# One SBUF arena, one PSUM pool and interleaved hand-overs between the four stages of a pre-LN recurrent-memory transformer block with its gradients

## The chip, the cores and the metric

The kernel runs on one core of a Trainium2 chip. The metric is the device time of one execution in microseconds (us), as the median of several executions; lower is better. A core has TensorE (PE; its weight loads are listed apart as PEld), VectorE (DVE), ScalarE (ACT), GpSimd (POOL) and SyncE (SP). They run their own instruction streams in order and meet at semaphores. SP and POOL also issue transfers (DMAs), which 16 DMA engines carry out.

## The reference

x is 2048 x 448, in bf16. A pre-normalised attention with a recurrent memory is followed by a gated feed-forward network (FFN), and the outputs are the result and the gradients for x, the first memory and seven weights:

```python
for s in range(n_seg):                       # 64 segments of 32 tokens, memory of 8 rows
    h = jnp.concatenate([mem, xs], axis=1)   # 40 rows
    q, k, v = h @ Wq, h @ Wk, h @ Wv         # 16 heads of 256
    p = softmax(mask(q k^T * scale))
    o = (p v) @ Wo
    mem = o[:, :M, :]                        # next segment needs this one
h = x + A(layernorm(x))
h2 = h + (silu(n @ w_gate) * (n @ w_up)) @ w_down      # n = layernorm(h)
# out: h2, and the vjp of all of it for grad_out
```

The memory makes the attention a chain over 64 segments forward and 64 segments backward.

## The kernel before

One scheduler mode is used throughout: the program's text is the order of each engine's instructions. The work has four stages, one after the other.

- **Forward** (`forward_chain`): 64 segments s, grouped by four into 16 token tiles t of 128 rows. Each segment projects K, Q and V (L471, L479), shifts V into the layout of the attention (V_sb, through POOL copies at L437 and SP transfers from Vev at L667), and multiplies by Wo (L600). A tile's output steps (o_units: u1, e1, u2, u3, e3, ut, et) are spread over the following segments; `out_ev` stores a tile of h (Hh, L653).
- **FFN**, forward and backward of it together (`ffn_phase`): 16 tiles t. Per tile: load h and grad_out, `norm`, `hn_turn` (L978), `gate`, `up`, `slope`, turn z (L1036), `dz` (dout times w_down transposed, L996 with its 64-row rest L999), `down_mm` (L1050), `grads`, `dh_turn` (L1036), `dh_mm` (L1079, both halves of the gradient of the normalised input), `dh_ln` and `dh_out` (L1096). `mm_d` works in pairs of 448-column banks: three chunks of 128 rows, then the last 64 rows from two halves of the partitions.
- **Backward** (`backward_chain`): segments 63 down to 0, with do_units (L1191) per tile and projections by the transposed weights WvT, WkT, WqT (L1218). WoT and WvT are loaded during the FFN, WkT and WqT (`load_back`, L926) after segment 63's own loads.
- **Tail** (`tail_phase`): 22 phases of weight gradients (L1674, L1689), six for the FFN and 16 for attention, with memory turns (`mem_turn`: load memld, transpose at L1663, store) inside the first two phases.

Big weights live in `wall`, four regions W[0] to W[3] that the stages reuse. Every stage opens its own SBUF pools and its own PSUM pool (6 banks + 2 fixed in forward and backward, 8 banks in FFN and tail), and is written out wholly before the next one begins.

The FFN's weights for its backward half come by `load_rest`, called at the head of `ffn_phase`. It is all on SP's queue, in this order: w_down (Wd, L905), three transposes of 128 columns of w_down (L907), a transpose of the last 128 columns (L908), a copy that puts the last 64 of them at partitions 0 to 63 of the fourth chunk (L909), then the transposes of w_gate (L910) and w_up (L911).

Of the kernel before, what the change touches and what calls it, by code (L numbers as in the profile page):

```python
# [18 lines left out]
class _Prio:  # L19
# [5 lines left out]
    def crit(self):  # L25
        from contextlib import contextmanager

        @contextmanager
        def _cm():
            off = self.tc.cur_priority - self.next  # L30
            with self.tc.high_priority(offset=off):
                yield
                self.next = self.tc.cur_priority
        return _cm()

# [147 lines left out]
def run_all(k: _K):  # L183
# [89 lines left out]
    with tc.tile_pool(name="wfwd", bufs=1) as wf, \  # L273
            tc.tile_pool(name="psA", bufs=6, space=bass.MemoryType.PSUM) as psa, \
            tc.tile_pool(name="psS", bufs=1, space=bass.MemoryType.PSUM) as pss:
        k.pspool = psa
        k.s_ps = [pss.tile([P, 512], FP32, name=f"s_ps{i}") for i in range(2)]
        for i in range(2):
            nc.vector.memset(k.s_ps[i][:], 0.0)
        Wk_sb, Wq_sb, Wv_sb = [W[i].rearrange("p (c n) -> p c n", c=KC) for i in range(3)]  # L280
        Wo_sb = W[3][:, 0:MC * D].rearrange("p (c d) -> p c d", c=MC)
        NWIN = 8
        hA = wf.tile([P, KC, NWIN, SEG], BF16)
        memT_all = W[3][:, MC * D:KC * HD].rearrange("p (c s m) -> p c s m", c=KC, s=NSEG)
        k.memT_all = memT_all
        maskf = wf.tile([L, L], FP32)
        nc.gpsimd.memset(maskf[:], 0.0)
        nc.gpsimd.affine_select(out=maskf[:], in_=maskf[:], compare_op=ALU.is_ge, fill=-1e9 / k.scale,
                                base=0, pattern=[[-1, L]], channel_multiplier=1)
        nc.gpsimd.memset(maskf[0:M, :], 0.0)  # L290
        maskr = wf.tile([L, H // 2 * L], BF16)
        for hh in range(H // 2):
            nc.vector.tensor_copy(out=maskr[:, hh * L:(hh + 1) * L], in_=maskf[:])
        k.part = wf.tile([P, DP], FP32, name="part")
        k.partB = wf.tile([P, DP], FP32, name="partB")
        nc.vector.memset(k.part[:], 0.0)
        nc.vector.memset(k.partB[:], 0.0)

        with tc.tile_pool(name="workA", bufs=2) as work, tc.tile_pool(name="stageA", bufs=1) as stage:
            order = ExitStack()  # L300
            order.enter_context(tc.manual_schedule())
            DB = D // 4
            m0f = work.tile([P, DP], BF16, name="m0", tag="xtmp", bufs=2)
            m0 = m0f[0:M, :]
            nc.sync.dma_start(out=m0[:, 0:D], in_=MEM0)
            Xs = W[3][:, 0:NT * D].rearrange("p (t d) -> p t d", t=NT)
            XNs = W[3][:, NT * D:2 * NT * D].rearrange("p (t d) -> p t d", t=NT)
            xv = X2.rearrange("(t p) d -> p t d", p=P)
            xnv = XN.rearrange("(t p) d -> p t d", p=P)
            for q in range(4):  # L310
                nc.sync.dma_start(out=Xs[:, 4 * q:4 * q + 4, :], in_=xv[:, 4 * q:4 * q + 4, :])
            for Wt, Wsrc in ((Wk_sb, Wk2), (Wq_sb, Wq2), (Wv_sb, Wv2)):
                wv = Wsrc.rearrange("(a j p) n -> a p j n", a=2, j=2)
                for a in range(2):
                    nc.sync.dma_start(out=Wt[0:DB].rearrange("p (j a) n -> p j a n", a=2)[:, :, a, :], in_=wv[a])
            pm = ps1(BF16)
            for kc in range(KC):
                w0 = (kc % 2) * 2 * DB + (kc // 2) * DB
                nc.tensor.transpose(pm[0:DB, kc * M:(kc + 1) * M], m0[:, w0:w0 + DB], ident[0:M, 0:M])
            k.evac(hA[0:DB, :, 0, 0:M], pm[0:DB, 0:KC * M].rearrange("p (c m) -> p c m", m=M), "v")  # L320
            nc.scalar.copy(out=memT_all[0:DB, :, 0, :], in_=hA[0:DB, :, 0, 0:M])
            mv1 = small.tile([P, NT, 2], FP32, name="mv1", bufs=1)
            sd1 = small.tile([P, NT], FP32, name="sd1", bufs=1)

            def norm_rows(out, t):
                nc.vector.tensor_scalar(out=out, in0=Xs[:, t, :], scalar1=mv1[:, t, 0:1], scalar2=rstd1[:, t:t + 1],
                                        op0=ALU.subtract, op1=ALU.mult)

            def first_rows(t):
                xl = work.tile([P, DP], BF16, name="xload", tag="xload", bufs=1)  # L330
                norm_rows(xl[:, 0:D], t)
                return xl

            def norm_group(q):
                ts = range(4 * q, 4 * q + 4)
                for t in ts:
# [7 lines left out]
            def store_group(q):  # L344
                for t in range(4 * q, 4 * q + 4):
                    norm_rows(XNs[:, t, :], t)
# [60 lines left out]
def forward_chain(k: _K, hA, NWIN, Wq_sb, Wk_sb, Wv_sb, Wo_sb, maskr, work, stage, ff):  # L407
# [289 lines left out]
    for s in range(NSEG):  # L697
# [44 lines left out]
        if s == NSEG - 1:  # L742
            ff.load_first()
# [186 lines left out]
def ffn_phase(k: _K, W, ff, work, mv2, rstd2, srcs):  # L930
# [194 lines left out]
    for t in range(NT):  # L1125
        if t + 2 < NT:
            load(t + 2)
# [715 lines left out]
```

## Time and profile before

| | us |
|---|---|
| median of 3 executions | 3030.61 (3029.78 to 3058.03) |
| the profiled execution's own time | 3044.81 |
| its span in the profile | 3043.0 |
| TensorE busy in that span | 2775.7 (91%) |
| VectorE, ScalarE, GpSimd busy | 1501.9, 1164.3, 737.2 |

The profiled execution was 14.2 us longer than the median; 1.8 us of it lie outside the span. Its mean granted TensorE clock was 0.971 of full speed.

The windows view, cut at the stages and at the seams between them (window, length, busy time and instruction count of each engine, granted TensorE clock, busy share of the DMA engines, GB/s):

```profile
65.00:980.00 915.00, 864.63 (x17644) 500.54 (x17640) 536.28 (x1683) 424.81 (x1130) 216.42 (x463) 0.99 0.40 125
980.00:1045.00 65.00, 39.63 (x384) 19.67 (x373) 25.78 (x58) 24.54 (x48) 8.14 (x15) 0.79 0.93 247
1045.00:1110.00 65.00, 62.71 (x436) 32.54 (x435) 47.38 (x80) 35.64 (x61) 16.27 (x25) 0.97 0.79 177
1110.00:1290.00 180.00, 180.00 (x1289) 95.76 (x1288) 138.12 (x234) 109.47 (x188) 38.11 (x72) 1.00 0.32 116
1345.00:1410.00 65.00, 31.75 (x474) 16.16 (x471) 17.99 (x44) 13.73 (x38) 7.98 (x18) 0.66 0.92 200
1410.00:2310.00 900.00, 846.88 (x19553) 485.11 (x19549) 533.66 (x1425) 430.53 (x1414) 228.11 (x466) 0.99 0.58 159
2310.00:2395.00 85.00, 67.40 (x684) 34.86 (x685) 16.73 (x44) 13.41 (x35) 24.62 (x43) 0.96 0.88 310
2395.00:3043.00 648.00, 615.31 (x3614) 310.85 (x3648) 123.01 (x233) 71.00 (x104) 175.33 (x241) 0.98 1.04 194
```

The first number after the length is TensorE (PE), then PEld, DVE, ACT, POOL. The stages proper are lines 1, 4, 6 and 8; lines 2, 5 and 7 are the seams forward to FFN, FFN to backward and backward to tail, and line 3 is the FFN's first tiles. In a timeline line the columns are start, length, engine, source line, operation, output and inputs, count, and in brackets the idle time before it with what ended it. The page's list of queues gives the queue of SP's transfers as a whole:

```profile
q1 hardware_dynamic: 577920, 297.58, 44.3%
```

That is packets, MB, and the time the packets took as a share of 16 engines' span.

### The profile page before, as it was taken

Reading aid. Unit: us, or ns where it says so; the run is one execution under the profiler, and the core shown is the slowest. Engines: PE = TensorE matmul, PEld = TensorE weight load, DVE = VectorE, ACT = ScalarE, POOL = GpSimd, SP = SyncE. Lnnn points to the kernel's source line nnn. Section 1 sums busy time; section 2 is a strip of 40 time slices with the busy share of each in tenths; the row PEclk is TensorE's granted clock in tenths of the full one; section 3 lists DMA queues with packets and bytes.
Section 4 is the critical chain, followed back from the end, with each engine's and each line's share of the span. In section 5 each row is a group of like instructions: output and inputs, shape, how many; then the busy total and the mean of one; then the engine's idle time right before and its main releaser. Section 6 shows DMA issues by size and latency. Waiting matters only on the chain.

```text
span 3043.0 us, 105017 instructions
## 1 busy us (share of the span) xinstructions
PE 2775.7 (91%) x44548; PEld 1530.2 (50%) x44584; DVE 1501.9 (49%) x3931; ACT 1164.3 (38%) x3087; POOL 737.2 (24%) x1388
## 2 busy tenths in 40 slices
PE   3999999999998799986999999999997999998989
PEld 1555555555554355543555555555554454444544
DVE  3555655565555577763556655656553112111211
ACT  1444444444443456652444544544442011110100
POOL 1222222222222122221222222222222223322232
PEclk7999999999999899997999999999999999999999
DMA  9343444434444763358655665665576999999995
GB/s 252 113 129 122 129 125 126 128 123 129 129 125 141 205 157 119 123 151 178 176 144 146 183 158 150 181 160 142 149 194 227 287 211 213 194 207 188 188 199 119
DMA packets 626771, 496.14 MB, mean 163 GB/s; under 512 B 487168, under 2 KB 538960, under 8 KB 616768
## 3 DMA queue, kind: packets, MB, share of 16 engines
q1 hardware_dynamic: 577920, 297.58, 44.3%
q0 software_dynamic: 48384, 191.85, 19.5%
q8 instruction: 352, 5.77, 0.8%
q14 instruction: 115, 0.94, 0.1%
HBM read 137.63 MB, written 222.08 MB: 118 GB/s over the span
## 4 chain that ended last, share of the span: by engine, by line
PE 71%; DMA 8%; DVE 7%; issue 6%; SPq 3%; ACT 3%; POOL 1%; another core or an unknown queue 0%; POOLq 0%; ACTq 0%; DVEq 0%
PE psf L1689 12%; PE psf L1218 9%; PE psf L471 9%; PE psf L1191 4%; PE psf L600 4%; DMA V_sb<-Vev 3%; PE psf L479 3%; PE psf L1494 3%; PE psf L1674 3%; PE psf L996 3%; PE psh L485 2%; PE psf L1702 2%; PE psf L1079 2%; DMA wall<-in_A_Wv_dram 2%; PE pob L1218 2%
## 5 line engine op out<-in xcount | busy, mean ns | idle before, releaser
L1689 PE MATMUL psf<-wall,H_all 128*128 128x512 bf16 x1404 | 322.1, 382 | 17.2 <-DMA wall<-dQA 11.7
L471 PE MATMUL psf<-wall,hA 112*32 112x512 bf16 x4096 | 233.4, 380 | 17.0 <-DVE hA L529 15.2
L1689 PEld LDWEIGHTS <-H_all 128*128 128x128 bf16 x1440 | 139.8, 98 | 183.2 <-issue 27.3
L1601 DVE CAST resc<-psf 128x512 bf16<-128x512 f32 (+1 forms) x58 | 39.0, 673 | 322.9 <-PE psf L1689 288.8
L471 PEld LDWEIGHTS <-hA 112*32 112x32 bf16 x4096 | 103.5, 97 | 129.8 <-DVE hA L529 31.3
L1599 ACT CAST resc<-psf 128x512 bf16<-128x512 f32 (+1 forms) x54 | 31.0, 573 | 334.4 <-PE psf L1689 297.0
L1545 POOL COPY dmem<-dA 128x32 bf16<-128x32 bf16 x63 | 13.2, 210 | 558.6 <-DVE dA L1230 558.6
L437 POOL COPY V_sb<-Vev 32x512 bf16<-32x512 bf16 x128 | 77.2, 603 | 275.1 <-ACT Vev L434 271.3
L1182 DVE COPY partC<-psf 128x224 f32<-128x224 f32 x64 | 25.0, 391 | 230.6 <-ACT partC L1185 230.6
L1191 PE MATMUL psf<-wall,dA 128*32 128x512 bf16 x2048 | 122.4, 381 | 13.0 <-DVE dA L1230 13.0
L1674 PE MATMUL psf<-dOut_all,wall 128*128 128x448 bf16 x640 | 127.1, 358 | 7.6 <-DMA wall<-OTA 7.6
L479 PE MATMUL psf<-wall,hA 112*32 112x512 bf16 x2048 | 134.0, 382 | 0.0
L1674 PEld LDWEIGHTS <-wall 128*128 128x128 bf16 x864 | 84.5, 99 | 95.9 <-issue 14.3
L1218 PE MATMUL psf<-wall,dkA 128*32 128x448 bf16 x2048 | 113.8, 364 | 18.6 <-DMA wall<-in_A_Wk_dram 13.1
L1218 PE MATMUL psf<-wall,dqA 128*32 128x448 bf16 x2048 | 113.2, 362 | 14.9 <-DMA wall<-in_A_Wq_dram 10.6
L1182 DVE COPY dO_sb<-dOev 32x512 bf16<-32x512 bf16 x256 | 121.2, 474 | 7.0
L1218 PE MATMUL psf<-wall,dvA 128*32 128x448 bf16 x2048 | 122.2, 358 | 0.4
L600 PE MATMUL psf<-wall,oA 128*32 128x224 bf16 x4096 | 116.7, 269 | 0.0
L1218 PE MATMUL pob<-wall 128*32 128x448 bf16 x1536 | 108.1, 358 | 1.7 <-issue 1.7
L1185 ACT CAST dOev<-psf 128x512 bf16<-128x512 f32 x64 | 37.5, 585 | 183.2 <-PE psf L1191 182.0
L1185 ACT CAST wall<-psf 128x64 bf16<-128x64 f32 x512 | 106.7, 247 | 0.0
L471 PE MATMUL psf<-wall,hB 112*32 112x512 bf16 x1024 | 75.6, 397 | 30.1 <-DMA wall<-in_A_Wk_dram 18.6
(284 smaller groups left out, 5792.5 us busy)
## 6 DMA issues: line engine op xcount, KB each, us to landing
Vtok<-V_sb SPq DMA_DIRECT2D x128, 192.0 KB
KtokA<-Kev SPq DMA_DIRECT2D x64, 256.0 KB
QtokA<-Qev SPq DMA_DIRECT2D x64, 256.0 KB
OTA<-oA POOLq DMA_DIRECT2D x16, 1024.0 KB, 6.0
Q_sb<-QtokA SPq DMA_DIRECT2D x128, 128.0 KB
K_sb<-KtokA SPq DMA_DIRECT2D x128, 128.0 KB
dVA<-dvA POOLq DMA_DIRECT2D x16, 1024.0 KB, 5.1
dKA<-dkA POOLq DMA_DIRECT2D x16, 1024.0 KB, 7.3
```

The source lines that it names most:

```text
L437: nc.gpsimd.tensor_copy(out=out, in_=in_)
L471: nc.tensor.matmul(ps[32 * g:32 * g + 32, :], lhsT=stat(kc), rhs=W_sb[0:DB, kc, c0:c0 + HB], start=(kc == 0), stop=(kc == KC - 1))
L479: nc.tensor.matmul(ps[32 * g:32 * g + 32, :].rearrange("t (y d) -> t y d", y=2), lhsT=stat(kc), rhs=wv[:, x, :, half, e, :], start=(kc == ...
L600: nc.tensor.matmul(ps[32 * g:32 * g + 32, 0:2 * DB], lhsT=x, rhs=Wo_sb[:, c, a * 2 * DB:(a + 1) * 2 * DB], start=first, stop=last)
L996: nc.tensor.matmul(out[b][:, 0:BW], lhsT=xT[:, kc, :], rhs=Wx[:, kc, f0:f0 + BW], start=(kc == 0), stop=False)
L1182: nc.vector.tensor_copy(out=out, in_=in_)
L1185: nc.scalar.copy(out=out, in_=in_)
L1191: nc.tensor.matmul(ps[32 * g:32 * g + 32, :], lhsT=stat(kc), rhs=WoT_sb[:, kc, c0:c0 + HB], start=(kc == 0), stop=(kc == KC - 1))
L1218: nc.tensor.matmul(pO[32 * g:32 * g + 32, 0:D], lhsT=ch(c), rhs=WT[:, c, :], start=(first and i < 4), stop=(last and i >= MC - 4), skip_gr ...
L1494: nc.tensor.matmul(po[:, n * L:(n + 1) * L], lhsT=lhs[b:b + L, lc:lc + P], rhs=rhs[b:b + L, hh, 0:L], start=True, stop=True)
L1674: nc.tensor.matmul(ps[:, 0:D], lhsT=stat[:, i, c * P:(c + 1) * P], rhs=Y[:, i, 0:D], start=(i == 0), stop=(i == kts - 1))
L1689: nc.tensor.matmul(ps[:, 0:N], lhsT=Hx[:, i, dc * P:(dc + 1) * P], rhs=X[:, i, b * N:(b + 1) * N], start=(i == 0), stop=(i == kts - 1))
```

## The change

**One arena.** All stages' buffers are views of one SBUF tile of 77,824 bytes per partition, at offsets written out as text per stage; a buffer waits only for those it overlaps. There is one PSUM pool of six rotating banks and two fixed ones (forward's scores; the FFN's pf and pdh; backward's scores and pob). FFN and tail so have 6 rotating banks instead of 8. The FFN's sg, u and z get two buffers, and slope works in place.

**Stages as generators.** `ffn_phase` is stepped from inside forward's last segment (`next(feed)`), backward from the FFN's last tiles (`next(back)`), and the tail from backward's last segment (`next(tails)`).

```diff
+        final = s == NSEG - 1
+        if final:
+            next(feed)                       # load(0), load(1)
...
-        v_shift(V_sb, Vev, 0, (2, 3), D_)
+        v_shift(V_sb, Vev, 0, (2, 3), A if final else D_)
...
-        v_shift(V_sb, Vev, 1, (0, 1), D_)
+        v_shift(V_sb, Vev, 1, (0, 1), G_ if final else D_)
...
         p_ev(1, 1, V)
+        if final:
+            next(feed)                       # rstd(0, NT - 1), norm(0)
...
             nc.sync.dma_start(out=dr["Vtok"][s, gg], in_=V_sb[QB * gg:QB * gg + 48, :])
+        if final:
+            next(feed)                       # load_rest
...
             if half == 1:
                 cur["u3"]()
+                if final:
+                    next(feed)               # hn_turn(0)
...
-    late2["et"]()
-    late["ut"]()
-    late["et"]()
-    u = o_units(NT - 1)
-    for n in ("u1", "e1", "u2", "u3", "e3", "ut", "et"):
-        u[n]()
+    uo["e3"]()
+    next(feed)                               # gate(0), first pair
+    uo["ut"]()
+    next(feed)                               # gate(0), second pair
+    uo["et"]()
```

The remarks behind the steps are added here. u1, u2 and u3 of the last tile now come right after segment 63's `ut`; its Hh is stored by POOL.

**load_rest.**

```diff
-        nc.sync.dma_start(out=self.Wd, in_=Wd2.rearrange("(c p) d -> p c d", p=P))
         for kc in range(full):
             nc.sync.dma_start_transpose(out=self.WdT[:, kc, :], in_=Wd2[:, kc * P:(kc + 1) * P])
-        nc.sync.dma_start_transpose(out=self.WdT[:, full, :], in_=Wd2[:, D - P:D])
-        nc.sync.dma_start(out=self.WdT[0:rem, full, :], in_=self.WdT[P - rem:P, full, :])
+        for h in range(2):
+            nc.sync.dma_start_transpose(out=self.WdT[rem * h:rem * (h + 1), full, :], in_=Wd2[:, D - rem:D])
+        nc.sync.dma_start(out=self.Wd, in_=Wd2.rearrange("(c p) d -> p c d", p=P))
         nc.sync.dma_start_transpose(out=self.WgT, in_=k.aps["B_w_gate"])
         nc.sync.dma_start_transpose(out=self.WuT, in_=k.aps["B_w_up"])
```

Here rem is 64 and full is 3. In the built program, each of the two new calls of 64 columns is a plain copy over 64 x 1792 x 1 elements; the calls of 128 columns are DMA transposes, as before.

**FFN to backward.** The tiles run in the order 0 to 13, 15, 14. The last two run stage by stage, and WvT, WkT and WqT are loaded in parts among them:

```diff
+    p, q = ORD[NT - 2:]                       # 15, 14
+    turn_f(T[p].z, ff.zT, (A, A))
+    dz(p)
+    dh_ln(p - 2)
+    down_mm(p)
+    grads(p)
+    dh_out(p - 2)
+    down_ev(p)
+    dout_turn(q)
+    turn_f(T[q].z, ff.zT, (A, A))
+    dz(q)
+    load_back(k, WT["k"], srcs["k"], False, 0, HC)
+    down_mm(q)
+    down_ev(q)
+    next(back)                                # Q, K and P of segment 63
+    load_back(k, WT["k"], srcs["k"], False, HC, 2 * HC)
+    dh_turn(p)
+    grads(q)
+    dh_mm(p)
+    dh_ln(p)
+    dh_turn(q)
+    dh_mm(q, (0,))
+    dh_out(p)
+    next(back)                                # backward's first tile
+    load_back(k, WT["q"], srcs["q"], False, 0, 14)
+    dh_mm(q, (1,))
+    load_back(k, WT["q"], srcs["q"], False, 14, 2 * HC)
+    dh_ln(q)
```

gate and up of tile 14 come before dh_turn(13), with WvT's halves loaded behind them. vT of segments 63 and 62 is loaded at tile 10; doutT of tile 14 stays in SBUF; `dh_out(14)` runs inside segment 63; segment 63's dO_sb is moved by POOL's queue.

**Backward to tail.** GO_all is loaded in segment 0 after the last outer product; HN_all is loaded behind phase 2's rows; memld gets five buffers instead of two, and a memory turn's TensorE step comes three units after its load instead of two:

```diff
+        if s == 0:
+            next(tails)                       # GO_all
...
-                at(i + 2, lambda box=box: box["pe"]())
+                at(i + 3, lambda box=box: box["pe"]())
+        if p == 0:
+            HN_all = work.tile([P, NKT, D], BF16, name="HN_all", tag="h2")
+            load_rows(HN_all, dr["HN"], 1)
```

More of the change, by code (lines that the diff above doesn't have):

```diff
@@ new lines @@
+dout_ld#0:1024x2
+du:3584 dgp:3584 dz:3584 scr:3584
+sg#0:3584 g#0:3584 u#0:3584 sg#1:3584 g#1:3584 u#1:3584
+doutT:1024x2
+z:3584x2 hnT:1024x2"""
+BWD = """dkA:8192 dqA:8192 dXl:1024 dmem:256x2
+P_b:1024x2
+dvA:8192 dOev:2048 dO_sb:4096
+doT:2560 prod:1280 dS:640 dST:640 partC:2048 partD:2048 dxnT:2048x3 dOBev:2048x2 doTB#0:2048
+dA:2048
+K_sb:4096 Q_sb:4096 dBx:256x2 doTB#1:2048 vT:3072x3"""
+TAIL = """h2:14336 memld#0:1024x3
+@17920 resr:896x3 memy:896x2 resc:2048x3 ldb:2048x4 dxn_ld:2048x2 xn_ld:896x2 dh_ld:1792x2 stb:2048x3 dx_b:896x2
```

811 lines of the change are left out of this document (443 added, 368 removed).

## The prediction

> **What bounds the kernel now.** I read the page's engine shares first (TensorE busy 2775.7 of 3043.0 us), then the windows in the table above, then TensorE's timeline where a window is not full. Inside the stages there is little: the forward window has 864.63 of 915 busy, ten feed-forward (FFN) tiles 180.00 of 180. The holes are where one stage ends and the next begins. TensorE's timeline at the first seam (start, length, what, idle before and its releaser):
>
> ```profile
> 990.26 0.43 PE L816 MATMUL psf<-PT,V_sb 104*128 104x80 bf16 x4 [5.94 <-DMA V_sb<-Vev]
> ...
> 1005.96 0.58 PE L978 MATMUL psh<-ident,hn 128*128 128x128 bf16 x4 [4.74 <-DVE hn L970]
> ...
> 1018.18 0.54 PE L996 MATMUL psf<-wall,doutT 128*128 128x448 bf16 x2 [0.49 <-DMA wall<-in_B_w_down_dram]
> 1021.08 0.90 PE L996 MATMUL psf<-wall,doutT 128*128 128x448 bf16 x2 [2.36 <-DMA wall<-in_B_w_down_dram]
> 1025.90 0.55 PE L999 MATMUL psf<-wall,doutT 64*128 64x448 bf16 x2 [3.92 <-DMA wall<-wall]
> ...
> 1043.58 2.62 PE L1079 MATMUL psf<-wall 128*128 128x448 bf16 x13
> ```
>
> The waits in brackets are what a better hand-over can win. Three of them end on the transposed w_down, and the last on its 64-column rest. SP's own timeline shows how that comes:
>
> ```profile
> 1006.68 10.94 SPq L907 DMA_TRANSPOSE wall<-in_B_w_down_dram  x3
> 1017.67 2.08 SPq L908 DMA_TRANSPOSE wall<-in_B_w_down_dram  x1
> 1022.86 0.52 SPq L909 DMA_DIRECT2D wall<-wall  x1
> ```
>
> At the second seam TensorE waits for backward's weights, which are asked for only after segment 63's own loads:
>
> ```profile
> 1335.32 0.94 PE L1036 MATMUL psh<-ident,z 128*128 128x128 bf16 x14
> ...
> 1353.70 0.61 PE L1096 MATMUL psh<-ident,dh_b 128*128 128x128 bf16 x4 [3.91 <-DVE dh_b L946]
> 1356.96 3.61 PE L1191 MATMUL psf<-wall,dBx 128*32 128x512 bf16 x32 [2.65 <-DVE dBx L1362]
> ...
> 1385.42 3.18 PE L1218 MATMUL psf<-wall,dkA 128*32 128x448 bf16 x32 [13.07 <-DMA wall<-in_A_Wk_dram]
> 1399.15 3.18 PE L1218 MATMUL psf<-wall,dqA 128*32 128x448 bf16 x32 [10.55 <-DMA wall<-in_A_Wq_dram]
> ```
>
> The third seam costs least; its largest wait is this:
>
> ```profile
> 2342.24 4.29 PE L1674 MATMUL psf<-GO_all,wall 128*128 128x448 bf16 x12 [7.66 <-DMA memld<-memTd]
> ```
>
> **Part 1, the first seam without its new transfer.** Removed: the V_sb waits 5.94 + 1.16 + 0.45 (ACT and POOL copies of 0.3 to 0.6 us take the place of transfers that the chain of waits shows at 9.40 us), 0.51 + 0.45 + 0.32 around the last output steps, 4.74 + 0.80 before the first FFN tile, 0.49 + 2.36 + 3.92 for w_down's transpose, 1.81 for tile 2's rows: 23 us. The clock there is 0.74 to 0.79, so 39.63 us of work could run some 4 us faster. Against this stands one square root moved before the attention's evictions on ACT, with a table load (1.28 + 0.31 us). Sum -25.
>
> **Part 2, the new transfer.** load_rest drops the 128-column transpose (L908) and the 0.52 us copy (L909) for two calls over w_down's last 64 columns, [1792 x 64] into [64 x 1792]. The built program holds no transpose for these but two plain copies, 64 x 1792 x 1, whose source steps 448 elements per element: 2 x 114,688 runs of two bytes, 14,336 on each of the 16 DMA engines, on SP's queue. Behind them queue w_down itself, the gate and up transposes and the loads of tiles 2 and 3; in front of TensorE, dz(0) needs both. Nothing covers them: gate(0), up(0), the turns of z, dout and hn are done by then, as in the timeline (1015.03 to 1017.15). So the question is the time T of 229,376 tiny runs. No such transfer is in the trace. The nearest rows, from the trace's packet records on that queue (size, time each, per engine):
> - 4 bytes: 9.9 ns (semaphore writes, 34,072 of them): T = 14,336 x 9.9 = 142 us.
> - A line through 128 bytes (12.9), 896 (41) and 2048 (84) gives about 8.1 ns at two bytes: 116 us.
> - 256 bytes: median 18, mean 25.5 ns: 258 and 366 us.
>
> In the window 1032.5 to 1037, where that queue alone runs small packets without a gap, the DMA view gives
>
> ```profile
> DMA packets 5093, 1.30 MB, mean 290 GB/s; under 512 B 5093, under 2 KB 5093, under 8 KB 5093
> ```
>
> so 5093 / 4.5 = 1132 packets per us, and T = 229,376 / 1132 = 203 us. I take 203: it is a sustained rate rather than a record's length, and lies between the 4-byte and 256-byte ends. A bound from below by bytes alone (459 KB at 290 GB/s) would be 1.6 us.
>
> The Trainium skill ("DMA: Bandwidth & Descriptors", DMA Transpose (X-bar), Constraints) says that an input smaller than a hardware tile, below 128 in its free dimension, can fall back to a rearranged access pattern with inefficient descriptors. That speaks against this edit; no run so far shows its price. Its Rules for kernel authors put such a copy at 19 times the hardware transpose.
>
> Where T enters: the copies start after three transposes (3 x 1792 packets at 1132 per us, 4.7 us, and landing) that now follow segment 63's stores at about 986.4, so near 994. After the landing come what stood between 1025.90 and 1043.58, 17.7 us, plus about 4 for w_down itself (now behind: 1792 packets x 41 ns / 16 = 4.6 us plus landing, part of it beside dz) and the low clock after idling. dh_mm(0) then starts at 994 + T + 22 = 1016 + T against 1043.58: seam one changes by **T - 28** (at T = 0 about part 1's sum), +175 at T = 203. Behind the waiting dz(0) stands all of TensorE's program; ACT's evictions of dz and DVE's grads(0) wait for it, and SP, which lets eight transfers be in flight, holds back tile 3's load until the copies land. None of these has other work to fill the time.
>
> **Part 3, the FFN steady state.** PSUM's rotating banks go from 8 to 6; two fixed ones hold pf and pdh. In the built order only the turn of hn two tiles ahead meets a bank late: its bank is free at 1229.11 in the trace, TensorE is there at 1228.97, so 0.14 to 0.2 us per tile, 14 tiles: **+2.6**. Doubled sg and the in-place slope cost nothing: DVE is busy 138.12 of 180.
>
> **Part 4, the second seam.** From 1335.32 the work left is, from the timeline: the last tile's own matmuls to the end of dh_mm, 13.8; do_units, 4.5; from L1191's end to partC's turn one steady segment's 12.8. Without waits, partC turns at 1366.4 instead of 1402.78: 36.4 us. Running the last two tiles stage by stage lets one tile's TensorE work lie over the other's DVE chain (the 3.91 and 2.65 waits), and halves of WvT, WkT, WqT (7168 packets, 6 to 8 us each) go into regions that the FFN has left. What is late next: WqT's last part, only free after dh_mm's second half; dO_sb of segment 63 on POOL's queue, behind the DH and DHb stores; and e3 on DVE behind dh_ln(14). I allow 5 us for these: **-31** (-24 to -36).
>
> **Part 5, the third seam.** GO_all is asked for at segment 0, before the last stores, HN_all (8.47 us on SP) moves behind phase 2's load, and memory turns come one step later with five buffers: 7.66 + 0.43 + 1.19 + 2.04 + 1.10 + 0.67 + 0.31 = 13.4, less about 1 for a first step that DMA still bounds (0.90 busy, 314 GB/s there): **-12** (-7 to -14).
>
> **Sum.** T - 28 + 2.6 - 31 - 12 = T - 68. On the profiled run's 3044.81 that is +135 at T = 203, 3180; the median of the runs shown is 14.2 lower, so the forecast on its basis is 3030.6 + 135 = **3165**.
>
> **Rivals.**
> - *The tiny runs are cheap*, or are not issued as tiny runs at all. If an engine walks a strided row inside one descriptor, or packs runs, T is bounded by other work. For it: 2-byte elements are 1/128 of a 256-byte packet, and the window's 1132 per us may be the transpose's own limit rather than that of small packets. Against it: every record on this queue is one contiguous run. At T between 2 (bytes) and 38 the time is 2965 to 3000, **faster**; the point where it decides is T = 68, 4.7 ns per run, half of the 4-byte row. The skill's factor 19, on 1792 packets / 1132 = 1.6 us for the same bytes, would be an estimate of 30 us, hence about 2993. Chance 0.12.
> - *Cancelled*: T from 38 to 98, 2.7 to 6.8 ns per run, within 1%. No row lies there: 0.06.
> - *Reads bound it*: each two-byte run touches its own piece of HBM, and 25.5 ns or more holds; T over 330, time above 3290. Chance 0.14.
> - *The six banks bind*: if each FFN tile loses 1 us rather than 0.2, 14 us on top. It decides nothing alone; it is in the range, as is a second seam worth only 24.
>
> **How the numbers follow.** T - 68 between 98 and 330 has chance 0.68, and its likeliest value is 3165. The range 3050 to 3310 takes in T = 90 to 345, from under the fitted line to near the 256-byte mean, with the seams' own few us. Measurements of this kernel tell 1% (30 us) from no change. Faster 0.12, same 0.06, slower 0.82.
>
> **What would show it.** After: two records from w_down of 64 x 1792 on SP's queue, some 229,000 more packets, and one TensorE wait of about 180 us or more at dz(0), ended by w_down, with the granted clock low after it; forward, backward and tail windows unchanged within 3 us; seam two without the 13.07 and 10.55 waits; seam three without 7.66. If the packet count does not rise, or that wait is under 40 us, part 2 is wrong and the kernel is faster.

## The result and the profile after

The changed kernel takes 3301.69 us (median of four, 3287.97 to 3349.03), the kernel before 3031.7 (3029.78 to 3058.03); the ratio is 1.0872 (95% interval 1.0831 to 1.0912). The profiled execution took 3291.37 us with a span of 3289.4, 246.4 more than the span before. The 3349.03 belongs to a disturbed execution and is not in the ratio.

The page of the changed kernel, by 40 slices of 82 us each:

```profile
PE   4999999999983000999989999999999899989998
PEclk9999999999996555999989999999999999989999
DMA  8343433433439999734675565655656799999996
...
q1 hardware_dynamic: 805120, 297.04, 57.1%
```

The 13th to 16th digits (987 to 1316 us) stand out: TensorE is idle, its granted clock goes down, and yet the DMA engines are never free. The windows view for that stretch (columns as in the table of before) says the same in numbers: 31.89 us of TensorE work in 330, a DMA share of 1.78 (records overlap), and 34 GB/s.

```profile
980.00:1310.00 330.00, 31.89 (x387) 17.72 (x376) 20.60 (x51) 17.90 (x36) 11.57 (x21) 0.54 1.78 34
```

TensorE's timeline there:

```profile
996.78 0.61 PE L1057 MATMUL psh<-ident,arena 128*128 128x128 bf16 x4 [2.32 <-DVE arena L1049]
...
1016.31 0.61 PE L1057 MATMUL psh<-ident,arena 128*128 128x128 bf16 x4 [1.86 <-DVE arena L1049]
...
1161.96 0.53 PE L1078 MATMUL psf<-wall,arena 64*128 64x448 bf16 x1 [141.70 <-DMA wall<-in_B_w_down_dram]
1310.71 0.53 PE L1078 MATMUL psf<-wall,arena 64*128 64x448 bf16 x1 [148.22 <-DMA wall<-in_B_w_down_dram]
...
1315.00 5.31 PE L1130 MATMUL s_ps<-wall 128*128 128x448 bf16 x14 [0.92 <-DMA wall<-in_B_w_down_dram]
...
1334.38 1.65 PE L1116 MATMUL psh<-ident,arena 128*128 128x128 bf16 x14 [7.15 <-DVE arena L1101]
...
1336.68 5.70 PE L1158 MATMUL s_ps<-wall 128*128 128x448 bf16 x28
```

Two waits of 141.70 and 148.22 us, both ended by w_down. They stand at the 64-row rest of dz(0): the first copy serves one half of the partitions, the second the other. The other lines are the seam's remaining waits: 2.32 and 1.86 us for DVE ahead of the copies, 0.92 for Wd behind them, and 7.15 for the DVE instructions that make tile 1's z. DVE itself had waited 6.76 us for tile 2's rows, which queue behind w_gate and w_up. SP's own queue shows the same two copies as one group, and what stands behind them:

```profile
1002.01 9.49 SPq L988 DMA_TRANSPOSE wall<-in_B_w_down_dram  x3
1011.59 144.53 SPq L990 DMA_DIRECT2D wall<-in_B_w_down_dram  x2
1156.22 149.01 SPq L991 DMA_DIRECT2D wall<-in_B_w_down_dram  x1
1305.34 12.93 SPq L992 DMA_TRANSPOSE wall<-in_B_w_gate_dram  x1
```

SP was held at w_down itself (L991) until 1305.23, when the second copy was all but done, and w_gate's transpose stood behind that. The prediction expected SP to be held only further on, at tile 3's load. In ten microseconds in the middle of it the DMA view gives

```profile
DMA packets 7980, 0.02 MB, mean 2 GB/s; under 512 B 7980, under 2 KB 7980, under 8 KB 7980
...
q1 hardware_dynamic: 7980, 0.02, 195.0%
```

7980 packets of two bytes in 10 us: 798 per us over 16 engines, 20.1 ns from one run to the next on each. By the packet records, 229,376 of them lie between 1015.5 and 1306.9 us, 291 us, and one takes 38 ns; nearly two are under way on each engine (195%). The queue as a whole has 227,200 packets more than before, as the prediction's signs asked.

At the second seam the waits for WkT and WqT are gone, and smaller ones have come:

```profile
1648.50 0.61 PE L1400 MATMUL psh<-ident,arena 128*128 128x128 bf16 x4 [3.46 <-DVE arena L1307]
...
1656.86 0.27 PE L1630 MATMUL psf<-arena 40*128 40x40 bf16 x4 [1.75 <-DMA arena<-arena]
1657.36 0.27 PE L1630 MATMUL psf<-arena 40*128 40x40 bf16 x4 [0.23 <-DMA arena<-arena]
...
1659.48 0.79 PE L1630 MATMUL psf<-arena 40*128 40x40 bf16 x24 [1.86 <-DMA arena<-arena]
```

At the third seam the wait of 7.66 us became this one, with three of some 0.4 us behind it, and none for memld is left:

```profile
2607.37 0.92 PE L1809 MATMUL psf<-arena,wall 128*128 128x448 bf16 x4 [1.40 <-DMA arena<-in_grad_out_dram]
```

Stretches between the same instructions of TensorE show where the time went. From segment 63's K projection to tile 0's dh_mm is the first seam; "partC" is the first turn of the backward's sums in segment 63, "partD" the last one; the tail's own stretch begins with the first matmul on HN_all. Wide transpose and last chunk first are two experiments below; the wide transpose was profiled twice.

| stretch, us | before | changed | wide transpose, twice | last chunk first |
|---|---|---|---|---|
| start to segment 63's projection | 974.91 | 982.17 | 975.30, 981.14 | 978.50 |
| projection to dh_mm(0): seam 1 | 68.67 | 354.51 | 62.45, 63.49 | 56.78 |
| dh_mm(0) to dh_mm(12) | 246.16 | 243.96 | 246.66, 244.34 | 245.96 |
| dh_mm(12) to partC: seam 2 | 113.04 | 90.22 | 92.08, 93.14 | 91.14 |
| partC to partD: backward | 930.83 | 934.14 | 931.50, 931.57 | 934.26 |
| partD to HN_all: seam 3 | 61.55 | 48.15 | 51.99, 48.21 | 49.62 |
| HN_all to the end of the last matmul | 641.29 | 629.71 | 641.82, 624.07 | 636.65 |

Changed against before the rows give +7.3, +285.8, -2.2, -22.8, +3.3, -13.4 and -11.6, in sum +246.4, the whole difference of the spans. The first and last rows differ as much between two profiles of the same kernel (975.30 and 981.14; 641.82 and 624.07), so they can't be put down to the change; over all twelve profiles with the changed forward stage the first row goes from 971.99 to 991.07.

### The profile page after: what moved, and what is told of

It reads as the page before. It is cut to its first block, busy times and chain, and to the rows that moved or that the text cites. A ratio compares the mean times of both kernels' runs of the same rounds, so it can differ in the third digit from the quotient of the medians.

```text
span 3289.4 us, 104977 instructions
## 1 busy us (share of the span) xinstructions
PE 2780.4 (85%) x44584; PEld 1536.7 (47%) x44584; DVE 1505.8 (46%) x3931; ACT 1164.0 (35%) x3091; POOL 741.6 (23%) x1393
## 4 chain that ended last, share of the span: by engine, by line
PE 40%; DVE 5%; issue 3%; DMA 2%; ACT 1%; SPq 1%; POOL 1%; DVEq 0%; POOLq 0%; ACTq 0%
PE psf L1824 11%; PE psf L1344 8%; PE psf L1316 4%; PE psf L1809 3%; PE psf L1630 3%; PE psf L1837 2%; PE s_ps L1344 1%; PE s_ps L1608 1%; PE psf L1351 1%; PE psh L1322 1%; PE psh L1657 1%; DVE arena L1612 1%; DVE arena L1618 1%; DVE arena L1615 1%; PE psh L1786 1%
## 5 line engine op out<-in xcount | busy, mean ns | idle before, releaser
L1824 PE MATMUL psf<-wall,arena 128*128 128x512 bf16 (+1 forms) x1824 | 398.0, 376 | 12.0 <-DMA wall<-dKA 12.0
L502 ACT CAST arena<-psf 128x512 bf16<-128x512 f32 (+2 forms) x560 | 235.8, 452 | 391.9 <-PE psf L539 138.4
L1344 PE MATMUL psf<-wall,arena 128*32 128x448 bf16 x6144 | 337.9, 361 | 11.2 <-issue 10.8
L539 PE MATMUL psf<-wall,arena 112*32 112x512 bf16 x5120 | 310.0, 385 | 43.7 <-DVE arena L597 20.8
L1310 ACT CAST arena<-psf 128x256 bf16<-128x256 f32 (+1 forms) x592 | 231.8, 419 | 262.6 <-PE psf L1316 187.9
L1824 PEld LDWEIGHTS <-arena 128*128 128x128 bf16 x1824 | 176.8, 98 | 215.4 <-issue 25.1
L499 DVE CAST arena<-psf 128x512 bf16<-128x512 f32 (+2 forms) x432 | 192.1, 469 | 136.5 <-PE psf L539 83.0
L1307 DVE CAST arena<-psf 128x256 bf16<-128x256 f32 (+1 forms) x336 | 162.6, 484 | 78.1 <-PE psf L1630 43.4
L547 PE MATMUL psf<-wall,arena 112*32 112x512 bf16 x2560 | 169.2, 385 | 9.8 <-DMA wall<-in_A_Wv_dram 9.8
L1316 PE MATMUL psf<-wall,arena 128*32 128x512 bf16 x2560 | 162.6, 384 | 15.3 <-DVE arena L1356 15.0
L1809 PE MATMUL psf<-arena,wall 128*128 128x448 bf16 x864 | 168.4, 353 | 5.5 <-DMA wall<-OTA 2.9
L1075 PEld LDWEIGHTS <-arena 128*128 128x128 bf16 x576 | 50.7, 99 | 200.8 <-issue 165.0
```

Source lines behind the costliest of these rows:

```text
L499: nc.vector.tensor_copy(out=out, in_=in_)
L502: nc.scalar.copy(out=out, in_=in_)
L539: nc.tensor.matmul(ps[32 * g:32 * g + 32, :], lhsT=stat(kc), rhs=W_sb[0:DB, kc, c0:c0 + HB], start=(kc == 0), stop=(kc == KC - 1))
L547: nc.tensor.matmul(ps[32 * g:32 * g + 32, :].rearrange("t (y d) -> t y d", y=2), lhsT=stat(kc), rhs=wv[:, x, :, half, e, :], start=(kc == ...
L1307: nc.vector.tensor_copy(out=out, in_=in_)
L1310: nc.scalar.copy(out=out, in_=in_)
```

## The experiments

**The element-wise copies undone.** The changed kernel with one edit:

```diff
-        for h in range(2):
-            nc.sync.dma_start_transpose(out=self.WdT[rem * h:rem * (h + 1), full, :], in_=Wd2[:, D - rem:D])
+        nc.sync.dma_start_transpose(out=self.WdT[:, full, :], in_=Wd2[:, D - P:D])
+        nc.sync.dma_start(out=self.WdT[0:rem, full, :], in_=self.WdT[P - rem:P, full, :])
```

> The changed kernel with one edit undone: the last 64 columns of w_down come by the 128-column transpose and the copy of before again, at the same place in load_rest. Theory: the two element-wise copies are the whole loss. Their packets fill 1015.5 to 1306.8 us of the trace, 291 us; a transpose and a copy of about 7 us take their place, so about 284 less than the changed kernel's 3301.69, that is near 3015, and 10 to 40 us under before's 3031.7 if the hand-overs gain what their landmarks show (-2 in the FFN, -23, -13 at the seams, +7 in forward). Rival, the arena and six banks cost something that the long wait hid: the time stays above 3031. Second rival, the copies only took the place of other waits: less than 200 us come back.

2998.38 us, 0.9892 of before (0.9842 to 0.9942). The whole loss was in these two lines, and the rest of the change is a gain of about 1%; neither of the two rivals in the expectation holds. Seam 1 with the wide transpose (start, length, instruction, the wait before it):

```profile
989.50 0.61 PE L1057 MATMUL psh<-ident,arena 128*128 128x128 bf16 x4 [3.09 <-DVE arena L1049]
...
1001.82 0.61 PE L714 MATMUL psh<-ident,arena 112*128 112x112 bf16 x4 [1.95 <-DVE arena L597]
...
1009.18 0.50 PE L1057 MATMUL psh<-ident,arena 128*128 128x128 bf16 x4 [1.86 <-DVE arena L1049]
...
1013.73 0.36 PE L1078 MATMUL psf<-wall,arena 64*128 64x448 bf16 x2 [0.57 <-DMA wall<-wall]
...
1019.11 4.49 PE L1130 MATMUL s_ps<-wall 128*128 128x448 bf16 x14 [3.48 <-DMA wall<-in_B_w_down_dram]
...
1035.45 1.65 PE L1116 MATMUL psh<-ident,arena 128*128 128x128 bf16 x14 [4.93 <-DVE arena L1101]
```

The two waits of over 140 us are gone. What is left of the seam's waits is spoken of below.

**The copies alone, in the kernel before.** load_rest there takes the changed kernel's two calls in place of L908 and L909 (the same diff the other way round).

> The kernel before with load_rest's new body alone. Theory: the two copies stand in front of dz(0) there too and nothing covers them: about 291 less 7 for the transpose and copy replaced, 3031.7 + 270 to 290 = 3300 to 3320, slower even than the changed kernel. Rival, the price comes from moving load_rest into forward's last segment (other transfers beside it): under 200 us are added.

3314.31 us, 1.0947 of before (1.0878 to 1.1015): 286 more than the 3028.0 of before on that chip, with the same pair of waits in the old place:

```profile
1168.91 0.53 PE L999 MATMUL psf<-wall,doutT 64*128 64x448 bf16 x1 [145.15 <-DMA wall<-in_B_w_down_dram]
1311.14 0.53 PE L999 MATMUL psf<-wall,doutT 64*128 64x448 bf16 x1 [141.69 <-DMA wall<-in_B_w_down_dram]
```

So neither the arena nor the hand-overs are needed for the loss.

**One copy of the two.** The second half of the partitions is copied from the first in SBUF.

```diff
-        for h in range(2):
-            nc.sync.dma_start_transpose(out=self.WdT[rem * h:rem * (h + 1), full, :], in_=Wd2[:, D - rem:D])
+        nc.sync.dma_start_transpose(out=self.WdT[0:rem, full, :], in_=Wd2[:, D - rem:D])
+        nc.sync.dma_start(out=self.WdT[rem:P, full, :], in_=self.WdT[0:rem, full, :])
```

> The changed kernel with only one of the two element-wise copies; the second 64 partitions are copied from the first in SBUF. If the price goes by the number of runs, half of 291 us is left: one copy of 145 us, time near 3301.69 - 143 = 3159. If it is a fixed cost or a queue that is blocked by something else, the time falls by clearly more or less than 143 +- 15.

3153.03 us, 1.0414 of before (1.0349 to 1.0479), 149 less than the changed kernel. 114,688 records lie in 142.3 us, 37 ns each (median 39). The price goes with the number of runs.

**Near neighbours instead of far ones.** Is it HBM, where each element lies 896 bytes from the last?

```diff
+        near = k.aps["A_Wq"].rearrange("d h e -> d (h e)")[0:rem, 0:2 * k.F].rearrange("p (n two) -> p n two", two=2)[:, :, 0]
         for h in range(2):
-            nc.sync.dma_start_transpose(out=self.WdT[rem * h:rem * (h + 1), full, :], in_=Wd2[:, D - rem:D])
+            nc.sync.dma_start(out=self.WdT[rem * h:rem * (h + 1), full, :], in_=near)
```

> The changed kernel with two copies of the same shape, 2 x 114,688 runs of two bytes, whose source steps two elements (4 bytes) instead of 448 (896 bytes); they read Wq in place of w_down, so the last 64 rows of the transposed w_down are other numbers and the gradients differ. If each run's own price on a DMA engine sets T, T stays within 10% of 291 us and a record near 38 ns. If scattered reads of HBM set it, neighbouring elements share their pieces of HBM and T falls below 200 us.

3324.4 us in a single execution; the records fill 302.1 us, 38 ns each. With elements 4 bytes apart it is no cheaper, so scattered reads are not the price: the prediction's rival "reads bound it" falls, though its number was near (a time above 3290, which the changed kernel's 3301.69 is).

**Two queues.** The second copy goes by ACT's queue.

```diff
-        for h in range(2):
-            nc.sync.dma_start_transpose(out=self.WdT[rem * h:rem * (h + 1), full, :], in_=Wd2[:, D - rem:D])
+        nc.sync.dma_start_transpose(out=self.WdT[0:rem, full, :], in_=Wd2[:, D - rem:D])
+        nc.scalar.dma_start_transpose(out=self.WdT[rem:P, full, :], in_=Wd2[:, D - rem:D])
```

> The changed kernel with the second of the two element-wise copies issued from ACT's queue, so that both run at once. In the changed kernel they ran one after the other, 145 us each, a run of 38 ns and 20.3 ns from one to the next on each of 16 engines. If a queue waits for its own answers (latency, some two runs in flight per queue), the two queues overlap: both done 145 to 170 us after the start, total near 3160. If the DMA engine itself is busy 20 ns with each run, both end after about 290 us as before, total 3290 to 3310, and a record gets longer, up to 76 ns.

3176.86 us in a single execution. In the same ten microseconds as above:

```profile
DMA packets 15201, 0.03 MB, mean 3 GB/s; under 512 B 15201, under 2 KB 15201, under 8 KB 15201
...
q1 hardware_dynamic: 7601, 0.02, 94.8%
q10 hardware_dynamic: 7600, 0.02, 94.0%
```

Two queues bring 1520 packets per us where one brings 798, and a record takes 20 ns instead of 38. So the engines were not at their limit with one queue. What rises is not the number of runs under way, which is nearly two per engine in both (195% and 189%): each run is done in half the time. Both copies took 210 us from the first record to the last, more than the 151 that 1520 per us would need. ACT's copy began 28 us earlier (997.6 against 1025.7) and ran at some 310 per us from 1000 to 1020, beside w_down's transposes, which took 20.66 us on SP there (9.49 in the changed kernel; waits of 9.62 and 4.73 us on TensorE). And in the last 36 us the DMA share was only 0.29, which fits a few engines finishing alone.

The Trainium skill ("DMA: Bandwidth & Descriptors", Rules for kernel authors) says that spreading DMAs over the issuing engines doesn't help bandwidth. For these runs it did, 798 against 1520 per us; the measurement decides, for transfers of this kind.

**Size of a run.** Seven copies of 229,376 bytes each on SP's queue replace the two, with runs of 4 to 256 bytes:

```diff
+        wq = k.aps["A_Wq"].rearrange("d h e -> d (h e)")[0:rem, 0:2 * k.F]
+        for i, run in enumerate((2, 4, 8, 16, 32, 64, 128)):
+            near = wq.rearrange("p (n two r) -> p n two r", two=2, r=run)[:, :, 0, :]
+            h = i % 2
+            nc.sync.dma_start(out=self.WdT[rem * h:rem * (h + 1), full, :].rearrange("p (n r) -> p n r", r=run), in_=near)
```

> The changed kernel with the two copies replaced by seven of the same 229,376 bytes each, which read Wq at every second run and write runs of 4, 8, 16, 32, 64, 128 and 256 bytes (57,344 down to 896 runs); the last 64 rows of the transposed w_down are other numbers, so the gradients differ. It measures the price of a run by its size. If a run costs the same at every size up to 64 bytes, each copy takes half the time of the one before it, from 73 us at 4 bytes (20.3 ns x 3584 runs per engine) to 4.6 us at 64. If tiny writes are what is dear, the price per run falls with the size, to near the 12.9 ns that 128-byte records took in the trace of before. If bytes set it, all take the same time.

3047.74 us in a single execution. From the packet records, first start to last end; the 4-byte row by its steady rate of 1700 packets per us, the 2-byte row from the changed kernel. The copies of 128 and 256 bytes are over in 1.5 and 1.3 us and are left out.

| run, bytes | runs | time, us | ns per run and engine |
|---|---|---|---|
| 2 | 229,376 | 291.3 | 20.3 |
| 4 | 57,344 | 1700 per us | 9.4 |
| 8 | 28,672 | 17.6 | 9.8 |
| 16 | 14,336 | 8.3 | 9.3 |
| 32 | 7,168 | 4.1 | 9.2 |
| 64 | 3,584 | 2.9 | 12.8 |

From 4 to 32 bytes a run costs the same, 9 to 10 ns; a two-byte run on this queue costs twice that. The expectation had 20.3 ns for all of them: half right, a fixed price per run there is, but the two-byte run has its own.

**No neighbours in the same word.** Each copy is cut into its even and its odd elements, 4 x 57,344 runs:

```diff
         for h in range(2):
-            nc.sync.dma_start_transpose(out=self.WdT[rem * h:rem * (h + 1), full, :], in_=Wd2[:, D - rem:D])
+            dst = self.WdT[rem * h:rem * (h + 1), full, :].rearrange("p (n two) -> p n two", two=2)
+            src = Wd2[:, D - rem:D].rearrange("(n two) p -> p n two", two=2)
+            for par in range(2):
+                nc.sync.dma_start(out=dst[:, :, par:par + 1], in_=src[:, :, par:par + 1])
```

> The changed kernel with each of its two copies cut into two, one for the even and one for the odd elements of a row: 4 x 57,344 runs of two bytes, as many as before, on the same queue, but no two successive runs write into the same four bytes. So far two-byte runs went at 798 packets per us on one queue (38 ns each) and at 1520 on two, and four-byte runs at 1700 on one. If a run that writes the other half of the word just written has to wait for it, the rate rises to 1500 to 1700 here, the copies take 135 to 155 us instead of 291, and the time falls to 3145 to 3170. If any two-byte write is that dear, or one queue keeps too few small runs in flight, the rate stays near 800 and the time at 3290 to 3325.

3278.23 us in a single execution; the copies take 285.5 us and the rate is the old one:

```profile
q1 hardware_dynamic: 7957, 0.02, 194.9%
```

A run does not wait for the other half of its word. Why two bytes cost twice what four do, and why a second queue takes that away, stays open; whether it is the reading or the writing side was not tried.

**Seam 1 in another order.** On the wide-transpose version: w_down's first transposes ahead of the Vtok stores, Wd ahead of the copy, tile 2's rows ahead of w_gate and w_up, hn_turn(0) behind the attention's last half. The cut shows the calls alone, with remarks added:

```diff
+        if final:
+            next(feed)                       # three transposes of w_down
         for gg in range(2):
             nc.sync.dma_start(out=dr["Vtok"][s, gg], in_=V_sb[QB * gg:QB * gg + 48, :])
         if final:
-            next(feed)                       # load_rest
+            next(feed)                       # last transpose, Wd, copy, load(2), w_gate, w_up
...
             if half == 1:
                 cur["u3"]()
-                if final:
-                    next(feed)               # hn_turn(0)
...
+        if final:
+            next(feed)                       # hn_turn(0), behind both halves
```

> The wide-transpose version with the first seam put in another order: w_down's first three transposes ahead of segment 63's Vtok stores, Wd ahead of the copy, tile 2's rows ahead of the transposes of w_gate and w_up, and hn_turn(0) behind the attention's last half. In that version the stretch from segment 63's projection to dh_mm(0) is 62.45 us, with waits of 3.09, 0.57, 3.48 and 4.93 us. If the order of the queue makes these waits, they go and the stretch falls to about 52. If the DMA engines' traffic bounds the seam (busy 0.77 to 1.07 there), the waits move to the transposes of w_gate and w_up and the stretch stays above 57.

2998.98 us in a single execution, but seam 1 takes 76.86 us, 14 more than 62.45. Neither branch of the expectation has this. The three transposes, 9.06 us on SP in the wide-transpose version, now take

```profile
995.16 36.90 SPq L990 DMA_TRANSPOSE wall<-in_B_w_down_dram  x3
```

and dz(0) waits 7.72 and 6.97 us for them, and 8.26 for the 64-row copy that now stands behind Wd:

```profile
1026.68 0.91 PE L1079 MATMUL psf<-wall,arena 128*128 128x448 bf16 x2 [7.72 <-DMA wall<-in_B_w_down_dram]
1034.55 0.91 PE L1079 MATMUL psf<-wall,arena 128*128 128x448 bf16 x2 [6.97 <-DMA wall<-in_B_w_down_dram]
...
1045.08 0.55 PE L1082 MATMUL psf<-wall,arena 64*128 64x448 bf16 x2 [8.26 <-DMA wall<-wall]
```

The queues while the transposes crawl (1005 to 1010 us) are first; then the wide-transpose version at 1000 to 1005, where the transposes have the engines to themselves:

```profile
q0 software_dynamic: 84, 0.41, 44.9%
q1 hardware_dynamic: 229, 0.07, 26.2%
```

```profile
q1 hardware_dynamic: 4175, 1.05, 103.9%
```

229 packets, nearly all transposed, in 5 us beside POOL's traffic of 0.41 MB, against 4175 alone. It goes on like this from 1006 to 1034 us, 130 transposed packets per us beside 2.6 MB of POOL's, and POOL's transfers crawl too: Zt lands after 17.3 us, in the wide-transpose version after 3.1. That POOL's traffic is the cause is not shown. The wide-transpose version at 1005 to 1010 us has more of it in as short a time, and more than ten times the packets:

```profile
q1 hardware_dynamic: 2634, 0.66, 68.8%
q0 software_dynamic: 176, 0.57, 32.0%
```

**The gentle order.** The same without the first of these moves: w_down's transposes stay behind the Vtok stores.

> The wide-transpose version with the first seam's small moves alone (w_down's transposes stay behind the Vtok stores): Wd ahead of the copy, tile 2's rows ahead of the transposes of w_gate and w_up, hn_turn(0) behind the attention's last half. If in the other order it was the transposes put ahead of the stores, running beside POOL's transfers, that cost the time, the stretch from segment 63's projection to dh_mm(0) is at most 62.45 us here, and 52 to 58 if the waits of 3.09, 3.48 and 4.93 us were the queue's order; dh_mm(0) may then wait for w_up instead. If the traffic as a whole bounds the seam, it stays at 60 to 64. As a time: within 10 us of the wide-transpose version, 1% under before.

3001.68 us, 0.9895 of before (0.9858 to 0.9933). Seam 1 takes 59.59 us: better than 62.45, so the loss came from the transposes' place, but dz(0) now waits 8.14 us for the 64-row copy behind Wd:

```profile
1030.51 0.55 PE L1081 MATMUL psf<-wall,arena 64*128 64x448 bf16 x2 [8.14 <-DMA wall<-wall]
```

The waits had been in the order only in part. Those of 3.48 and 4.93 us went with Wd's and tile 2's places; the 3.09 in front of hn_turn(0) did not go with hn_turn's place (3.07 here).

> The wide-transpose version once more, on the same chip as the one before it, so that the two can be compared. About 0.989 of before, as in its first runs; its stretches (62, 247, 92, 931 and 52 us from segment 63's projection on) should come back within 2 us, except the tail's, whose waits for dKA, dQA and OTA differ from run to run (627 to 642 us so far).

The wide transpose on the same chip: 3003.78 us, 0.9914 (0.9885 to 0.9943). The two can't be told apart by time; the stretches in the table came back within 2.4 us, but for the start (5.8), seam 3 (3.8) and the tail (17.8).

**The last chunk first.** On the gentle order (the `yield`s that part load_rest are left out):

```diff
+        nc.sync.dma_start_transpose(out=self.WdT[:, full, :], in_=Wd2[:, D - P:D])
         for kc in range(full):
             nc.sync.dma_start_transpose(out=self.WdT[:, kc, :], in_=Wd2[:, kc * P:(kc + 1) * P])
-        nc.sync.dma_start_transpose(out=self.WdT[:, full, :], in_=Wd2[:, D - P:D])
-        nc.sync.dma_start(out=self.Wd, in_=Wd2.rearrange("(c p) d -> p c d", p=P))
-        nc.sync.dma_start(out=self.WdT[0:rem, full, :], in_=self.WdT[P - rem:P, full, :])
+            if kc == 1:
+                nc.sync.dma_start(out=self.WdT[0:rem, full, :], in_=self.WdT[P - rem:P, full, :])
+        nc.sync.dma_start(out=self.Wd, in_=Wd2.rearrange("(c p) d -> p c d", p=P))
```

> The gentle order once more, with w_down's last 128 columns transposed first of the four and their copy issued between the second and third of the others. In the gentle order dz(0) waited 8.14 us for that copy, which was issued at 1022.31 behind Wd; tile 0's dh_mm came 59.59 us after segment 63's projection. If the copy's place in the queue is what dz(0) waits for, that wait falls to 0 to 3 us and the stretch to 53 to 57; if the traffic of w_down as a whole is, the wait moves to the last plain transpose or to Wd and the stretch stays at 58 to 62. As a time: 0.985 to 0.990 of before.

2999.66 us, 0.9905 of before (0.9873 to 0.9937); seam 1 takes 56.78 us. The wait for the copy is gone, as expected, and smaller ones for w_down's transposes, for Wd (the second line) and for w_up, late now, have taken its place:

```profile
1015.70 0.54 PE L1079 MATMUL psf<-wall,arena 128*128 128x448 bf16 x2 [1.47 <-DMA wall<-in_B_w_down_dram]
...
1022.05 4.49 PE L1134 MATMUL s_ps<-wall 128*128 128x448 bf16 x14 [3.98 <-DMA wall<-in_B_w_down_dram]
...
1040.19 2.81 PE L1162 MATMUL s_ps<-wall 128*128 128x448 bf16 x14 [2.10 <-DMA wall<-in_B_w_up_dram]
```

This has the shortest first seam by the table, but its wait of 2.10 us lies just behind that stretch. Counted on to dh_mm(1) the seam is 88.85 us before, 83.90 and 84.42 with the wide transpose, 79.90 in the gentle order and 79.35 here, so the two orders are one. This version beats both kernels, as the wide transpose does; by time the three can't be told apart.

**WqT's second part later.** On the wide-transpose version, to free the engines for segment 63's dO_sb:

```diff
     dh_mm(q, (1,))
-    load_back(k, WT["q"], srcs["q"], False, 14, 2 * HC)
     dh_ln(q)
     yield
+    load_back(k, WT["q"], srcs["q"], False, 14, 2 * HC)
     dh_out(q)
```

> The wide-transpose version with WqT's second part asked for only inside segment 63, after dO_sb's transfers. There the projection waits 5.04 + 0.75 + 1.56 us for dO_sb, which were issued at 1352.90 to 1354.98 in the middle of WqT's transposes. If they wait for engines that the transposes hold, these waits fall to 2 to 3 us in sum and the stretch from the twelfth tile's dh_mm to partC's turn goes from 92.1 to about 88. If they wait for POOL's issue or the dOB copy on DVE, the waits stay; and a new wait for WqT at its first use would show that the time was only moved.

3025.59 us in a single execution; the stretch of seam 2 is 92.89 us, not 88. dO_sb's waits sum to 6.6 instead of 7.35 us, and WqT is late by 1.76 (waits in front of the first dO_sb product and of the projection by WqT):

```profile
1372.46 0.31 PE L1630 MATMUL psf<-arena 40*128 40x40 bf16 x4 [5.27 <-DMA arena<-arena]
...
1386.73 1.32 PE L1344 MATMUL psf<-wall,arena 128*32 128x448 bf16 x24 [1.76 <-DMA wall<-in_A_Wq_dram]
```

The second part was not what held them up. Whether WqT's first part is, which was issued just before them, was not tried. The longer time is hardly the edit's: against the wide transpose's profile this stretch is 0.8 us longer, the start up to segment 63 9 us.

## Why the prediction was right, and where it was off

The direction and its reason were right: part 2's two copies run element by element, nothing covers them, dz(0) waits, and all else is small beside it. 3301.69 lies inside the range of 3050 to 3310, 8 us from its end and 137 above the likeliest value. Of the signs, the packets, w_down as the releaser, the low clock (0.54) and the seams' vanished waits came as told. The one wait of 180 us came as two, one for each half of the partitions; forward, backward and tail did not stay within 3 us (+7.3, +3.3 and -11.6), though the first and last vary as much by themselves.

- **T, the price of the copies, was mis-sized.** 203 us were taken, from a sustained 1132 packets per us; 291 were measured, 798 per us. The step that failed is the choice of that rate: it is the rate of 256-byte transposed packets (14.1 ns each per engine), taken over for two-byte runs because it lay between the rows. Four-byte runs did cost 9.4 ns, but that this meets the 9.9 of the semaphore writes is chance: 9.9 is the length of a record, and a four-byte record of the size experiment takes 18 ns, with nearly two under way. Two bytes cost twice as much on one queue, which no row of before could show. The 256-byte row's median of 18 and mean of 25.5 ns, kept as the upper end, were nearer, by accident: the size table shows no such price for any run of 4 to 32 bytes.
- **Part 1, the first seam, was mis-sized too**: -25 forecast, -5 to -6 measured (68.67 to 62.45 and 63.49 with the wide transpose). Both errors of the sum go the same way, to a slower kernel. The waits for V_sb went (7.55 us), and so did those for w_down's transposes (0.49 + 2.36). But in the profile of the wide transpose others stand at their old places with another length: for hn 3.09 instead of 4.74, before the last output step's turn 1.95 instead of 0.32, for the 64-row copy 0.57 instead of 3.92, for tile 2's rows 4.93 instead of 1.81 (through DVE, which waits 4.54 for them; they are still behind w_gate and w_up). Two are new: 3.48 for Wd, which is now last, and 1.86 for tile 1's hn. That is 15.9 in sum. So TensorE's idle time in the stretch fell from 25.4 us to 18.2 and 21.5 only. The step that failed is that all 23 us of waits were counted as won, while the table showed the DMA engines 0.93 busy over this seam. The 4 us for a faster clock did not come either: the granted clock over the stretch was 0.80 before, and 0.80 and 0.79 with the wide transpose. The changed orders then showed that 4 to 5 us were the order's (to dh_mm(1)) and that a bad order costs 14 (76.86). Whether the DMA traffic as a whole makes the rest is not shown.
- **Where T enters** was put too early. In the changed kernel the first run of the copies came 33.3 us after segment 63's projection (1015.52 less 982.17), where the prediction had 19 (994 less 974.91): the stores and three transposes ahead of it end at 1011.50. Behind the copies dh_mm(0) came 29.8 us later, where it had 22. These 14 and 8 are what lies between T - 28 at the measured T, 263, and the measured 285.8.
- **Part 3** was right: a tile's period went from 20.18 to 20.31 us, 0.13 against the 0.14 to 0.2 forecast. The stretch of twelve tiles is 2.2 us shorter all the same, because the kernel before has one period of 24.18 in it.
- **Part 4** was over-sized: -31 forecast with -24 as the weak end, -20 to -23 measured. The waits for weights went; dO_sb by POOL's queue cost 7.35 us with the wide transpose (5.04 + 0.75 + 1.56) and 3.84 in the changed kernel, where 5 had been allowed for everything, and dh_out's turn still waits 2.64 to 3.46 for DVE.
- **Part 5** was right: -12 forecast, -9.6 to -13.4 measured.
- **The rivals.** Cheap runs (T below 68) are excluded: one copy alone took 142 us. The factor of 19 that the Trainium skill ("DMA: Bandwidth & Descriptors", Rules for kernel authors) gives for such a copy was far too low here: against 1.6 us for the same bytes as a transpose (an estimate, 1792 packets at 1132 per us), 291 us is 180 times. A copy that cancels the rest (T of 38 to 98) is excluded with them. Scattered reads are excluded by the near neighbours, six binding banks by part 3.

In the place of T - 68 the stretches show 292 (354.51 less 62.45) for the copies, less about 6, 22 and 12 at the three seams: +252, beside +246 between the two profiles and +264 by the ratio (0.0872 x 3031.7); what lies between these is about as much as the last row of the table differs from run to run (17.8).

## What to carry to other kernels

Look into the built program for what a call has become: a transpose of 64 columns was a copy of 114,688 two-byte runs, and that edit cost 292 us where the whole rest of the change gained some 26 to 33 (0.0086 x 3028.5 and 0.0108 x 3028.0). The price of such a transfer was the number of its runs times 9 to 20 ns per engine, not its bytes, for runs of 2 to 32 bytes from HBM on SP's queue. And don't add up the waits of a seam as if all could be won: here 15.9 of 23 us stayed or came back elsewhere, with the DMA engines 0.9 to 1.1 busy, so read that share and ask which transfer can start earlier.

## What was not expected of the hardware

- A two-byte run cost 20.1 ns per engine on one queue and 10.5 on two queues together (798 and 1520 per us), with nearly two runs under way per engine in both; runs of 4 to 32 bytes cost 9.2 to 9.8 ns on one.
- In one order of the first seam three DMA transposes took 36.90 us in place of 9.06, at 130 packets per us for 28 us, while POOL's transfers beside them crawled too; in another version 2634 packets went through in 5 us beside 0.57 MB of POOL's. What makes the difference stays open.
- After waits of 141.70 and 148.22 us TensorE ran slow only for a short while: the changed kernel's first down_mm took 5.31 us against 2.82 in the steady state, and six matmuls of gate(1), 9.4 us after TensorE went on, 1.30 as always. Most of this is not the long wait's: with the wide transpose the same down_mm took 4.49 us, after a wait of 3.48.
